# Beacon attention and soft MoE: V brought in four keys to a partition and put in order by matrix products

## The chip, the cores and the metric

The kernel runs on one core of a Trainium2 chip. The metric is the device time of one execution in microseconds (us); lower is better. Times are compared as medians of several executions.

## The reference

Attention comes first, for 8 batches and 8 heads of 576 queries with 64 elements each. 16 beacon keys, which every query sees, stand ahead of 576 causal keys. The result, as 4608 tokens of 512 elements, goes through a soft mixture of 8 experts with 4 slots each.

```python
k_all = np.concatenate([beacon_k, k], axis=2)          # 592 keys
v_all = np.concatenate([beacon_v, v], axis=2)
scores = scale * np.matmul(q, k_all.transpose(0, 1, 3, 2))
causal[:, Nb:] = np.triu(np.ones((S, S), dtype=bool), k=1)
a = np.exp(scores - scores.max(-1, keepdims=True)) ; a /= a.sum(-1, keepdims=True)
x = np.matmul(a, v_all)                                 # heads side by side: 4608 x 512
logits = x @ phi                                        # 4608 x 32 slots
d = softmax(logits, over tokens) ; slot_input = d.T @ x
slot_out[e] = np.maximum(slot_input[e] @ w1[e], 0.0) @ w2[e]
out = softmax(logits, over slots) @ slot_out
```

All inputs and the output are float32. Q, K, V and the beacons are 29 MB, the expert weights 33.5 MB, the output 9.4 MB.

## The kernel before

**Pairs.** The work is 32 pairs of heads, n = 0 to 31, four to a batch. g is n % 4 and b is n // 4. The order inside a pair is written out by hand: `order` (L472) gives a list of steps for each g, with other lists for the first two and the last three pairs, and `do` (L492) issues a step. S0 to S3 are the four steps of scores of a pair (`score`, L306). Each writes one of two PSUM buffers `sc0` and `sc1` in turn, and ScalarE takes the exponential of it into the tile `ex` (L319). S0 belongs to the next pair. A0 and A1 (`attend`, L334) multiply the exponentials of the pair before with V, for its two heads; after A1 VectorE takes the reciprocal of the sums (`r`, L348) and scales the result into `xb` (L349). T (`transp`, L284) transposes Q and K of pair n + 2 with 36 products of 64x64 into two buffers of the PSUM pool `tr`, which has two buffers in all; VectorE copies them out as `qT` and `kT` (L293). X01, X23 and X4 transpose `xb` of the batch before, L0 and L1 make its logits (L391, exponential on ScalarE at L395), D turns the exponentials (`dt_piece`, L425), SI sums the slots (L441, L454). All of these borrow buffers of `tr` as well.

**V.** `load_r` (L117) brings a batch's V in two loads of 128 partitions with two neighbouring keys to a partition, that is pieces of 512 bytes; the beacon rows are loaded over the first eight partitions (`load_bv`, L136) once the load below them has landed. The last 80 keys come on their own (`load_vl`, L140). GpSimd casts to float16 (`cast_r`, L354). Partition p of a chunk holds keys 2p and 2p + 1, so the scores read every other column of kT (`ks` in `steps`, L60), and the diagonal of the first 256 keys is folded: eight products of 64x64 in S0, a copy `vd` of half of V with zeros beside it (`dup`, L360, VectorE), two products per head against `vd` that are 130 columns wide, and a mask by a minimum with `fmask` (`mask_f`, step M, L331, VectorE). The other masks run on GpSimd (L303).

**Weights.** GpSimd issues 37 loads that cast to float16 (`load_w`, L156, issue at L171). `want(n)` (L540) says how many have been issued by the end of pair n: 0.68 n up to pair 24, and then a table. The last ten are halves that go into the buffers of Q and K when these come free.

**Start and queue.** SyncE issues the loads of Q and K of pairs 0 to 4, of the beacon keys, and of V at L181 to L200; later ones at L565 to L578. It works in order, and a load that has to wait holds up those behind it.

**End.** After the last pair come the logits of the last batch, the slot sums, layer one of two groups of four experts (`layer1`, L634), `turn` (L655), and layer two (`layer2`, L668) with 64 products of 512 columns that add up in one PSUM bank; 32 columns of weights at a time, so that four lie beside each other. Between the last pairs of products of layer two stand products whose result nobody reads (`idle_work`, L488, L688). Then `soh` (L690) is scaled, and 36 products, scalings and stores write the output (L695).

Of the kernel before, what the change touches and what calls it, by code (L numbers as in the profile page):

```python
# [17 lines left out]
def kernel(  # L18
# [13 lines left out]
    P = 128  # L32
# [21 lines left out]

    def f_(s):
        return [(64 * r, 64, 2 * P * r + s, 2, 2 * P * r, P, P * s) for r in range(2)]

    steps = [  # L60
        f_(0) + f_(1) + [(0, P, 2 * P, 2, 3 * P, U - 3 * P, 2 * P)],
        [(0, P, 2 * P + 1, 2, 3 * P, U - 3 * P, 0), (0, UL, 4 * P, 1, 4 * P, UL, 208)],
        [(0, P, 0, 2, P, U - P, 0)],
        [(0, P, 1, 2, P, U - P, 0)],
# [4 lines left out]
    XF, XG1, XT, XG0 = (0, P), (2 * P, 464), 672, (752, 1216)  # L69

    POS = [0, 2, 1, 3, 4]
    prods = [(P, XF[0], P, 0, 0, 2)] + [(P, XG0[s] + P, P, s, 1, 1) for s in range(2)]
    prods += [(P, XF[1], P, 1, 0, 2)]
    prods += [(P, XG0[s], P, s, 2, 1) for s in range(2)]
    prods += [(P, XG0[s] + 2 * P, P, s, 3, 1) for s in range(2)]
    prods += [(P, XG1[s], P, 2 + s, 3, 1) for s in range(2)]  # L80
    prods += [(P, XG0[s] + 3 * P, UL, s, 4, 1) for s in range(2)]
    prods += [(P, XG1[s] + P, UL, 2 + s, 4, 1) for s in range(2)] + [(UL, XT, UL, 4, 4, 1)]
    first, final = {0, 4, 6, 10}, {3, 5, 9, 14}
# [29 lines left out]

    vr, vl = {}, {}
    vrows = v.rearrange("b h s d -> (b h s) d")

    def load_r(b, r):  # L117
        t = vrp.tile([P, H, 2 * D], FP, name="vr", tag="vr")
        vr[(b, r)] = t
        o = b * H * S + 2 * P * r - Nb  # L120
        if b == 0 and r == 0:
            nc.sync.dma_start(
                out=t[:, 1:H, :], in_=vrows[S - Nb:S - Nb + (H - 1) * S].rearrange(
                    "(h s) d -> h s d", s=S)[:, 0:2 * P, :].rearrange(
                        "h (p t) d -> p h (t d)", t=2))
            nc.sync.dma_start(
                out=t[Nb // 2:P, 0, :],
                in_=v[0, 0, 0:2 * P - Nb, :].rearrange("(p t) d -> p (t d)", t=2))
        elif r == 0:
            nc.sync.dma_start(out=t[:, :, :], in_=vrows[o:o + H * S].rearrange(  # L130
                "(h s) d -> h s d", s=S)[:, 0:2 * P, :].rearrange("h (p t) d -> p h (t d)", t=2))
        else:
            nc.sync.dma_start(out=t[:, :, :], in_=v[b, :, 2 * P - Nb:4 * P - Nb, :].rearrange(
                "h (p t) d -> p h (t d)", t=2))

    def load_bv(b):  # L136
        nc.sync.dma_start(out=vr[(b, 0)][0:Nb // 2],
                          in_=beacon_v[b].rearrange("h (p t) d -> p h (t d)", t=2))
# [53 lines left out]
    load_bk(1, B)  # L192
    load_pair(2)
    load_r(0, 1)
    load_vl(0)
    load_bv(0)
# [13 lines left out]
    fmask = const.tile([P, 2 * P], F16, name="fmask")  # L210
    fm = const.tile([P, 2, P], F16, name="fm")
    nc.gpsimd.memset(fm[:, :, :], 65504.0)
    for base, lo in ((P, 64), (0, 0)):
        nc.gpsimd.affine_select(out=fm[:, :, :], in_=fm[:, :, :], compare_op=AL.is_ge,
                                fill=0.0, base=base, pattern=[[-1, 2], [1, P]],
                                channel_multiplier=-2)
        nc.gpsimd.tensor_copy(out=fmask[lo:lo + 64, :].rearrange("p (s t) -> p s t", s=2),
                              in_=fm[lo:lo + 64, :, :])
# [5 lines left out]
    for i in range(2):  # L224
        nc.gpsimd.memset(vh[i][:, :, :, D:DD], 1.0)


    vd = [const.tile([P, 2, 2, H, DD], F16, name=f"vd{i}") for i in range(2)]
    for i in range(2):
        nc.vector.memset(vd[i][:, :, :, :, :], 0.0)  # L230
    hTz = vd[0][:, :, :, :, :].rearrange("p s r h d -> p (s r h d)")
# [74 lines left out]
    def score(n, st):  # L306
        if st == 0:
            ex[n] = exq.tile([P, 2, EW], F16, name="ex", tag="ex")
        sc = scs[st % 2]
        for (p0, kn, k0, ks, u0, un, col) in steps[st]:  # L310
            for a in range(2):
                nc.tensor.matmul(  # L312
                    sc[p0:p0 + kn, a, col:col + un],
                    kT[n % 3][64 * a:64 * a + 64, k0:k0 + ks * (kn - 1) + 1:ks],
                    qT[n % 3][64 * a:64 * a + 64, u0:u0 + un],
                    start=True, stop=True)
        w, o = width[st], soff[st]
        x = ex[n]
        nc.scalar.activation(x[:, :, o:o + w], sc[:, :, 0:w], AF.Exp, scale=scale)  # L319

        if st == 0:
            mask(x[:, :, XG1[0]:XG1[0] + P], [[0, 2], [1, P]], P, -2)
        if st == 1:
            mask(x[:, :, XG1[1]:XG1[1] + P], [[0, 2], [1, P]], P - 1, -2)
            mask(x[0:UL, :, XT:XT + UL], [[0, 2], [1, UL]], 0, -1)
        if st >= 2:
            mask(x[:, :, XG0[st - 2]:XG0[st - 2] + P], [[0, 2], [1, P]], P + 2 - st, -2)

    def mask_f(n):
        x = ex[n][:, :, 0:2 * P]  # L330
        nc.vector.tensor_tensor(out=x, in0=x, in1=fmask[:, :].unsqueeze(1).broadcast_to(  # L331
            [P, 2, 2 * P]), op=AL.min)

    def attend(n, a):  # L334
        b, g = divmod(n, H // 2)
        h = 2 * g + a
        for j, (kn, o, m, c, pos, w) in enumerate(prods):
            dst = avs[0:m, a, pos * DD:(pos + w) * DD]
            if w == 2:
                dst, rhs = dst.rearrange("p (r d) -> p r d", r=2), vd[b % 2][:, c, :, h, :]  # L340
            else:
                rhs = vh[b % 2][0:kn, c, h, :]
            nc.tensor.matmul(dst, ex[n][0:kn, a, o:o + m], rhs,  # L343
                             start=j in first, stop=j in final)
# [9 lines left out]
    def cast_r(b, r, eng):  # L354
        eng.tensor_copy(  # L355
            out=vh[b % 2][:, 2 * r:2 * r + 2, :, 0:D].rearrange("p s h d -> p h s d"),
            in_=vr.pop((b, r))[:, :, :].rearrange("p h (s d) -> p h s d", s=2))

    def dup(b, r):
        nc.vector.tensor_copy(out=vd[b % 2][64 * r:64 * r + 64, :, r, :, :],  # L360
                              in_=vh[b % 2][0:64, 2 * r:2 * r + 2, :, :])
# [7 lines left out]
    def xt_piece(b, cs):  # L369
# [3 lines left out]
        for ii, i in enumerate(cs):  # L373
            m = P if i < 4 else UL
            for t in range(NDC):
                nc.tensor.transpose(  # L376
                    tp[:, ii, t, 0:m],
                    xb[b % 2][0:m, POS[i], 2 * t:2 * t + 2, :].rearrange("p h d -> p (h d)"),
# [23 lines left out]
    def xt_pair(g):  # L402
        tp = ps_tr.tile([P, NCH, P], F16, name="tr", tag="tr")
        for i in range(NCH):
# [3 lines left out]
                xb[(B - 1) % 2][0:m, POS[i], 2 * g:2 * g + 2, :].rearrange("p h d -> p (h d)"),  # L408
# [27 lines left out]
    def si_piece(b):  # L436
        sp = ps_tr.tile([P, NDC, NSL], FP, name="tr", tag="tr")
        for t in range(NDC):
            for i in range(NCH):
# [3 lines left out]
                    xb[b % 2][0:m, POS[i], 2 * t:2 * t + 2, :].rearrange("p h d -> p (h d)"),  # L443
# [6 lines left out]
    def si_moving(b):  # L450
        sp = ps_tr.tile([P, Dm], FP, name="tr", tag="tr")
        for i in range(NCH):
# [3 lines left out]
                xb[b % 2][0:m, POS[i], :, :].rearrange("p h d -> p (h d)"),  # L456
# [15 lines left out]
    order = ["d1 S1 A0 L1 M S2 A1 S3 cl T S0 D", "S1 A0 X01 M S2 SI A1 S3 T S0",  # L472
# [19 lines left out]
    def do(n, w):  # L492
# [32 lines left out]
        elif w[0] == "c" or w[0] == "d":  # L525
# [8 lines left out]
            else:  # L534
                dup(vb, int(w[1]))


    wl = 0

    def want(n):  # L540
# [203 lines left out]
```

## Time and profile before

| | |
|---|---|
| median of 3 runs | 213.84 us (213.62 to 214.66) |
| the profiled execution's own time | 214.08 us |
| its span, first to last instruction | 212.3 us |
| mean granted clock of TensorE | 0.955 |
| busy: PE, DVE, ACT, POOL | 166.0, 141.5, 127.4, 116.2 us |
| moved by DMA | 55.86 MB |

PE is TensorE, PEld its weight loads, DVE VectorE, ACT ScalarE, POOL GpSimd, SP SyncE; a q behind a name means the queue in front of the engine. A group line gives the line of the kernel, the engine, the operation, output and inputs, the number of instructions, then busy time and the mean of one in ns, and then the idle time ahead of it. The chain of waits is followed back from the last instruction; "issue" in it is time in which an engine waited for nothing that the profile shows. The durations of PE rows are latencies of a pipeline, so the time that a product takes from its neighbours is read from the starts, not from the durations.

### The profile page before, as it was taken

The page shows a single profiled execution, that of the slowest core. Times are in us where ns is not written, and L with a number is a line of the kernel's source. Part 1 is how long each engine was busy: PE and PEld are TensorE (multiplying, and loading weights), DVE is VectorE, ACT ScalarE, POOL GpSimd, SP SyncE. Part 2 cuts the span into 40 slices and gives each one's busy share as a digit, 9 for nine tenths or more (in the row PEclk, how much of TensorE's full clock was granted, in tenths as well). Part 3 has the DMA queues.
Part 4 walks back from the last instruction along what each step waited for, and adds up shares of the span by engine and source line. Part 5 has one row for each costly group of instructions (what it writes and reads, how often), then busy time and mean ns, then how long its engine had stood idle before and what let it go on. Part 6 is the DMA issues. An engine that isn't in the chain of part 4 may idle for free.

```text
span 212.3 us, 7656 instructions
## 1 busy us (share of the span) xinstructions
PE 166.0 (78%) x3276; PEld 110.7 (52%) x3276; DVE 141.5 (67%) x289; ACT 127.4 (60%) x179; POOL 116.2 (55%) x278
## 2 busy tenths in 40 slices
PE   2353999997899898689999789899899889888000
PEld 2232776765676576467666556666667542233000
DVE  5766489894798799279979678877855230299200
ACT  2154499795688778477978677688682210199100
POOL 7137179695658938556985676899887200000000
PEclk9999999996999999799999999999999999999855
DMA  6999899999999999999999999999999994089995
GB/s 191 294 267 342 275 286 277 275 278 280 299 246 285 269 266 305 298 282 290 296 271 242 289 287 260 244 209 212 211 211 212 210 209 75 0 297 415 415 412 240
DMA packets 44968, 55.86 MB, mean 263 GB/s; under 512 B 9103, under 2 KB 25991, under 8 KB 44935
## 3 DMA queue, kind: packets, MB, share of 16 engines
q1 hardware_dynamic: 36151, 38.60, 58.0%
q0 software_dynamic: 8784, 16.78, 42.5%
q8 instruction: 25, 0.41, 0.8%
q14 instruction: 8, 0.07, 0.1%
HBM read 62.71 MB, written 9.44 MB: 340 GB/s over the span
## 4 chain that ended last, share of the span: by engine, by line
PE 52%; DVE 15%; issue 8%; POOL 7%; DMA 6%; ACT 2%; SPq 1%; DVEq 0%; ACTq 0%; POOLq 0%
PE av L343 17%; PE sc L312 12%; PE tr L291 6%; DVE osb L708 4%; PE tr L391 4%; DVE xb L349 3%; DMA vr<-in_beacon_v_dram 3%; PE tr L376 3%; POOL ex L303 3%; DMA vr<-in_v_dram 3%; DVE qT L293 3%; PE av L671 3%; POOL vh L355 2%; PE sc L490 2%; POOL w L171 2%
## 5 line engine op out<-in xcount | busy, mean ns | idle before, releaser
L319 ACT ACTIVATE ex<-sc 128x928 f16<-128x928 f32 (+1 forms) x128 | 107.6, 869 | 42.0 <-PE sc L312 38.7
L303 POOL TENSOR_SCALAR_AFFINE_SELECT ex<-ex 128x256 f16<-128x256 f16 (+1 forms) x160 | 62.2, 406 | 44.1 <-ACT ex L319 42.7
L312 PE MATMUL sc<-qT,kT 64*64 64x128 bf16 (+3 forms) x576 | 52.4, 270 | 4.7 <-issue 2.7
L343 PEld LDWEIGHTS <-ex 128*128 128x128 f16 (+2 forms) x960 | 42.4, 109 | 16.7 <-issue 12.1
L343 PE MATMUL av<-vh,ex 128*128 128x65 f16 (+2 forms) x832 | 46.0, 202 | 0.7 <-issue 0.2
L312 PEld LDWEIGHTS <-kT 64*64 64x64 bf16 (+2 forms) x576 | 20.9, 104 | 18.9 <-issue 11.8
L349 DVE TENSOR_TENSOR xb<-av,r 128x640 f16<-128x640 f32 x32 | 26.4, 824 | 1.1
L343 PE MATMUL av<-vd,ex 128*128 128x130 f16 x128 | 23.4, 232 | 3.3 <-DVE vd L360 3.3
L293 DVE COPY kT<-tr 128x576 bf16<-128x576 bf16 x32 | 24.0, 748 | 2.0 <-PE tr L291 2.0
L293 DVE COPY qT<-tr 128x576 bf16<-128x576 bf16 x32 | 23.9, 748 | 1.6 <-PE tr L291 1.6
L291 PE MATMUL tr<-idb,kf 64*64 64x64 bf16 x576 | 16.4, 199 | 4.9 <-issue 4.2
L171 POOL DMA_DIRECT2D w<-in_moe_w_dram x27 | 19.4, 721 | 0.0
L291 PE MATMUL tr<-idb,qf 64*64 64x64 bf16 x576 | 16.2, 201 | 3.8 <-DMA qf<-in_q_dram 3.8
L705 ACT ACTIVATE osb<-fp,rc 128x512 f32<-128x512 f32 x18 | 11.3, 684 | 13.1 <-PE fp L703 12.4
L291 PEld LDWEIGHTS <-qf 64*64 64x64 bf16 x576 | 12.5, 114 | 10.2 <-issue 5.3
L355 POOL CAST vh<-vr 128x1024 f16<-128x1024 f32 x15 | 15.8, 1052 | 3.0 <-DMA vr<-in_beacon_v_dram 3.0
L331 DVE TENSOR_TENSOR ex<-ex,fmask 128x512 f16<-128x512 f16 x32 | 15.6, 487 | 2.6 <-ACT ex L319 2.3
L291 PEld LDWEIGHTS <-kf 64*64 64x64 bf16 x576 | 13.3, 115 | 5.6 <-issue 5.4
L381 DVE COPY xT<-tr 128x1024 f16<-128x1024 f16 x14 | 9.7, 691 | 7.3 <-PE tr L376 7.3
L348 DVE RECIPROCAL r<-av 128x10 f32<-128x10 f32 x32 | 6.9, 214 | 11.3 <-PE av L343 10.7
L360 DVE COPY vd<-vh 64x1040 f16<-64x1040 f16 x16 | 8.7, 543 | 6.4 <-POOL vh L355 6.2
L708 DVE TENSOR_SCALAR osb<-fp,rc 128x512 f32<-128x512 f32 x18 | 12.3, 746 | 0.7 <-PE fp L703 0.7
(90 smaller groups left out, 156.7 us busy)
## 6 DMA issues: line engine op xcount, KB each, us to landing
w<-in_moe_w_dram POOLq DMA_DIRECT2D x27, 512.0 KB, 9.4
qf<-in_q_dram SPq DMA_DIRECT2D x32, 288.0 KB, 7.0
kf<-in_k_dram SPq DMA_DIRECT2D x32, 288.0 KB, 7.5
out_dram<-osb SPq DMA_DIRECT2D x16, 512.0 KB, 5.5
vr<-in_v_dram SPq DMA_DIRECT2D x15, 512.0 KB, 7.3
wx<-in_moe_w_dram POOLq DMA_DIRECT2D x10, 256.0 KB, 9.7
vl<-in_v_dram SPq DMA_DIRECT2D x8, 160.0 KB, 7.0
out_dram<-osb SPq DMA_DIRECT2D x4, 256.0 KB, 3.2
```

Of the source, the lines that this page charges most:

```text
L171: nc.gpsimd.dma_start(out=t[:, 0:1024 * len(hs)].rearrange("p (c f) -> p c f", f=1024), in_=src)
L291: nc.tensor.transpose(tp[po:po + 64, j, :], hi, idb[po:po + 64, po:po + 64])
L293: nc.vector.tensor_copy(out=dst[:, Nb:Nb + S].rearrange("p (s j) -> p s j", j=J), in_=tp[:, :, :].rearrange("p j s -> p s j"))
L303: nc.gpsimd.affine_select(out=x, in_=x, compare_op=AL.is_ge, fill=0.0, base=base, pattern=pattern, channel_multiplier=cm)
L312: nc.tensor.matmul(sc[p0:p0 + kn, a, col:col + un], kT[n % 3][64 * a:64 * a + 64, k0:k0 + ks * (kn - 1) + 1:ks], qT[n % 3][64 * a:64 * a + ...
L319: nc.scalar.activation(x[:, :, o:o + w], sc[:, :, 0:w], AF.Exp, scale=scale)
L331: nc.vector.tensor_tensor(out=x, in0=x, in1=fmask[:, :].unsqueeze(1).broadcast_to([P, 2, 2 * P]), op=AL.min)
L343: nc.tensor.matmul(dst, ex[n][0:kn, a, o:o + m], rhs, start=j in first, stop=j in final)
L349: nc.vector.tensor_tensor(out=xb[b % 2][:, :, 2 * g:2 * g + 2, :].rearrange("p i a d -> p a i d"), in0=avv[:, :, :, 0:D], in1=r5[:, :, :]. ...
L355: eng.tensor_copy(out=vh[b % 2][:, 2 * r:2 * r + 2, :, 0:D].rearrange("p s h d -> p h s d"), in_=vr.pop((b, r))[:, :, :].rearrange("p h (s ...
L705: nc.scalar.activation(osb[:, j - j0, :], fp_[:, :], AF.Copy, scale=rc[:, i:i + 1])
L708: nc.vector.tensor_scalar(out=osb[:, j - j0, :], in0=fp_[:, :], scalar1=rc[:, i:i + 1], scalar2=None, op0=AL.mult)
```

## The change

V comes in four keys to a partition, half of the heads at a time (r is now the half): 60 and 64 partitions in two loads with pieces of 1 KB, and four partitions of beacons, which no longer overlap with the rest. The cast goes into a new tile `vc`. `v_order` takes it from there: for each of four chunks of 128 keys it adds up four products of 32 rows by 512 columns with the 0/1 tile `vsel`, two chunks in turn into the two buffers of `tr`, and VectorE (ScalarE for one of each two in pairs 0 and 1) copies them to `vh`. With the keys in order, the scores read kT without a stride, the mask M, `fmask`, `vd` and `dup` go, S0 has four products instead of ten, `attend` has fifteen products of 65 columns per head, and GpSimd has four masks a pair instead of five, the first twice as wide. In a batch's lists, c0 and c1 (casts) stand at g = 1 and 2 for the next batch, V01 at g = 3 between S2 and A1, V23 at g = 0 of the batch itself at the same place.

At the start V is loaded ahead of pair 2; the beacon keys of the other batches come after pair 2, and their cast and transposes (BC, BT) move from pair 0 to pair 1. Later loads of V are asked for by a table. `want` is one higher in most pairs up to 24. At the end, layer one and `turn` are interleaved, the unread products between the products of layer two go, `soh` is made in two halves, and the first output tile is made and stored in two halves. The diff, cut to its core:

```diff
     steps = [
-        f_(0) + f_(1) + [(0, P, 2 * P, 2, 3 * P, U - 3 * P, 2 * P)],
-        [(0, P, 2 * P + 1, 2, 3 * P, U - 3 * P, 0), (0, UL, 4 * P, 1, 4 * P, UL, 208)],
-        [(0, P, 0, 2, P, U - P, 0)],
-        [(0, P, 1, 2, P, U - P, 0)],
+        [(P, 0, 0, P, 0), (P, 2 * P, 2 * P, U - 2 * P, P)],
+        [(P, 3 * P, 3 * P, U - 3 * P, 0), (UL, 4 * P, 4 * P, UL, 208)],
+        [(P, 0, P, U - P, 0)],
+        [(P, P, P, U - P, 0)],
     ]
+    base = [soff[2] - P, soff[3] - P, P - 2 * P, soff[1] - 3 * P, soff[1] + 208 - 4 * P]
+    prods = [(j, c, 0 if j == 0 else base[c] + P * j) for j in range(NCH) for c in range(j + 1)]
...
     def load_r(b, r):
-        t = vrp.tile([P, H, 2 * D], FP, name="vr", tag="vr")
...
+        t = vrp.tile([P, HH, 4 * D], FP, name="vr", tag="vr")
+        hs_ = slice(r * HH, (r + 1) * HH)
+        for lo, hi in ((Nb // 4, 64), (64, P)):
+            nc.sync.dma_start(out=t[lo:hi, :, :], in_=v[b, hs_, 4 * lo - Nb:4 * hi - Nb, :]...)
+        nc.sync.dma_start(out=t[0:Nb // 4], in_=beacon_v[b, hs_]...)
...
     load_r(0, 0)
-    load_bk(1, B)
-    load_pair(2)
     load_r(0, 1)
     load_vl(0)
-    load_bv(0)
+    load_pair(2)
+    load_bk(1, B)
...
-    vd = [const.tile([P, 2, 2, H, DD], F16, name=f"vd{i}") for i in range(2)]
-    for i in range(2):
-        nc.vector.memset(vd[i][:, :, :, :, :], 0.0)
+    vc = const.tile([P, 4, H, D], F16, name="vc")
...
         if st == 0:
-            mask(x[:, :, XG1[0]:XG1[0] + P], [[0, 2], [1, P]], P, -2)
+            mask(x[:, :, 0:2 * P].rearrange("p a (i t) -> p a i t", i=2),
+                 [[0, 2], [0, 2], [1, P]], 0, -1)
+        if st == 1 or st == 3:
+            mask(x[:, :, o:o + P], [[0, 2], [1, P]], 0, -1)
...
+    def v_order(b, cs, engs):
+        tp = {c: ps_tr.tile([P, 512], FP, name="tr", tag="tr") for c in cs}
+        for t in range(4):
+            for c in cs:
+                nc.tensor.matmul(tp[c][:, :], vsel[32 * c:32 * c + 32, t, :],
+                                 vc[32 * c:32 * c + 32, t, :, :].rearrange("p h d -> p (h d)"),
+                                 start=t == 0, stop=t == 3)
+        for c, eng in zip(cs, engs):
+            o, i = vh[b % 2][:, c, :, 0:D], tp[c][:, :].rearrange("p (h d) -> p h d", d=D)
+            if eng is nc.scalar:
+                nc.scalar.activation(o, i, AF.Copy)
+            else:
+                eng.tensor_copy(out=o, in_=i)
...
-    order = ["d1 S1 A0 L1 M S2 A1 S3 cl T S0 D", "S1 A0 X01 M S2 SI A1 S3 T S0",
-             "S1 A0 X23 X4 M S2 A1 S3 c0 T S0", "d0 S1 A0 L0 M S2 A1 S3 c1 T S0"]
+    order = ["S1 A0 L1 cl S2 V23 A1 S3 T S0 D", "S1 c0 A0 X01 S2 SI A1 S3 T S0",
+             "S1 c1 A0 X23 X4 S2 A1 S3 T S0", "S1 A0 L0 S2 V01 A1 S3 T S0"]
-    lists[0] = "M BC S1 S2 BT c0 S3 d0 S0 cl".split()
-    lists[1] = "S1 M T0 c1 S2 d1 A0 S3 A1 S0 T".split()
+    lists[0] = "S1 c0 S2 c1 S3 V01 S0 cl".split()
+    lists[1] = "S1 V23 T0 S2 A0 S3 A1 S0 BC BT T".split()
+    lists[2] = "S1 A0 S2 c0 A1 S3 T S0".split()
+    lists[3] = "S1 A0 c1 S2 A1 S3 V01 T S0".split()
...
-            return int(0.68 * n)
+            return int(0.68 * n + 0.7)
...
-    hs0 = layer1(0)
...
+    for hf in range(2):
+        layer1(0, scs[0][:, hf, :], hf)
+    for hf in range(2):
+        relu(hs[0], scs[0][:, hf, :], hf)
+    layer1(1, hp1[0], 0)
+    turn(0, hs[0])
+    layer1(1, hp1[1], 1)
...
     for e in range(EG, E):
-        for t in range(0, NFC, 2):
-            layer2(e, (t, t + 1))
-            if e >= E - 2 and (e, t) != (E - 1, NFC - 2):
-                idle_work(spare, 2)
+        layer2(e, range(NFC))
...
-    nc.vector.tensor_scalar(out=soh[:, :], in0=sop[:, :], scalar1=rd[:, 0:1],
-                            scalar2=None, op0=AL.mult)
+    for hf in range(2):
+        nc.vector.tensor_scalar(out=soh[:, hf * HD:(hf + 1) * HD], in0=sop[:, hf * HD:(hf + 1) * HD],
+                                scalar1=rd[:, 0:1], scalar2=None, op0=AL.mult)
...
+                w = HD if i == 0 else Dm
+                for o in range(0, Dm, w):
...
```

## The prediction

> **What bounds the kernel now.** I read the page's slices first, then the busy time of four stretches, the chain of waits, one pair in the timeline, and the waits by engine.
>
> ```profile
> PEclk9999999996999999799999999999999999999855
> DMA  6999899999999999999999999999999994089995
> ```
>
> The transfers are at nine tenths or more from the second slice to about 177 us, pause for layer two, and are full again for the output. So the last weights, and behind them the output, can't come much earlier, whatever the engines do. Is that the only limit? The next answer, whose columns are the stretch, its length, busy time of PE, PEld, DVE, ACT and POOL, granted clock, DMA share and GB/s, has two mishaps and, in its last line, a batch without one.
>
> ```profile
> 47.40:48.90 1.50, 0.04 (x3) 0.00 (x0) 0.99 (x2) 0.50 (x1) 1.31 (x4) 1.00 1.11 261
> 49.70:53.10 3.40, 3.40 (x38) 2.35 (x36) 1.24 (x3) 2.75 (x5) 1.42 (x4) 0.50 1.11 279
> 84.20:86.90 2.70, 0.02 (x3) 0.01 (x2) 1.59 (x3) 0.03 (x1) 1.41 (x2) 1.00 1.09 359
> ...
> 53.60:70.26 16.66, 15.80 (x379) 11.47 (x379) 14.61 (x29) 13.89 (x20) 12.41 (x29) 1.00 1.10 285
> ```
>
> The clean batch takes 16.66 us with PE busy for 15.80, DVE for 14.61, ACT for 13.89: TensorE runs through its list with hardly a gap, VectorE is close behind. The other batches take up to 20.9 us, because PE stands still and then runs at half clock. The chain names it (start, length, what):
>
> ```profile
> 9.22 6.93 DMA vr<-in_beacon_v_dram
> ...
> 47.44 1.49 issue
> ...
> 84.22 2.68 issue
> ...
> 117.32 1.56 issue
> ...
> 177.69 0.54 PE sc L490 x2
> ```
>
> First the beacon rows of V hold up the start, then there are three stops that no semaphore explains, and from 177.69 the unread products carry the end. One pair (g = 2 into g = 3) in the timeline (start, length, engine, line):
>
> ```profile
> 98.69 0.37 PE L312 MATMUL sc<-qT,kT 64*128 64x464 bf16 x2
> ...
> 98.99 0.23 PE L343 MATMUL av<-vd,ex 128*128 128x130 f16 x1
> 99.06 0.22 PE L343 MATMUL av<-vh,ex 128*128 128x65 f16 x2
> ...
> 99.65 0.37 PE L312 MATMUL sc<-qT,kT 64*128 64x464 bf16 x2
> ...
> 101.06 0.13 PEld L312 LDWEIGHTS <-kT 64*128 64x128 bf16 x3 [0.17 <-issue]
> ...
> 102.58 0.41 ACT L395 ACTIVATE eLh<-tr 128x288 f16<-128x288 f32 x1
> 102.77 0.71 POOL L171 DMA_DIRECT2D w<-in_moe_w_dram  x1
> 102.78 0.23 PE L343 MATMUL av<-vd,ex 128*128 128x130 f16 x1
> ```
>
> S2 starts at 98.69 and A1 0.30 later, S3 at 99.65, and S1 of the next pair only at 101.06, 1.41 after S3, since it needs `sc1` back from the exponential of S3. In the waits, `PE tr L430 <- DVE qT L293: 3.2, 6, 0.5` shows that step D, at the end of g = 0, already stands half a microsecond for a `tr` buffer.
>
> **The change in the loop.** A batch gains V01 and V23, eight products of 512 columns each.
> - *Their streaming.* Four products of 288 columns take 0.49 (chain, PE tr L391 x4), so 512 columns take 0.218. S2's two products of 464 columns run side by side on 64 rows each: 0.198 of stream and 0.10 of changeover make the 0.30 above. If 32-row products pair up like that, a V is 4 x 0.218 + 0.10 = 0.97; one by one it is 8 x 0.218 + 0.10 = 1.84. The 64-row pair is the nearest row: 0.97.
> - *Their buffers.* V takes both buffers of `tr`, and the second belongs to L0 or L1, which stand just ahead. The logits' exponential starts at 102.58 and with its read of the sum ends at 103.08, while A1, where V would start, stood at 102.78. So the second chunk, and in order the rest, waits 0.3: V = 1.27, two make 2.5.
> - *VectorE.* M (487 ns) and dup (543) leave, 4 x 0.487 + 2 x 0.543 = 3.0 a batch; four copies of 128x512 from PSUM come, at the 692 ns of L651, 2.8. The sum is even, the place is not: both copies of a V stand ahead of `r` and `xb`, and A1 is only 0.6 long, so `r` comes some 0.6 late. A0 of the next pair has 0.46 of slack (xb over at 104.61, A0 at 105.07) and loses 0.1; D, which has none, loses 0.5. Together 0.6 a batch (0.1 to 1.4).
> - *What is saved.* A product against `vd` takes 0.07, one against `vh` 0.03 (98.99 to 99.06, then two to 99.12); two of 15 per head, so 0.12 a pair, 0.5 a batch (0.3 to 0.7). S0 falls from ten products to four, but T and S0 lie inside the 1.41 that ACT sets: nothing. GpSimd loses one mask in five and has one twice as wide (0.41, so 0.41 to 0.82), its casts keep their 1.05; with 12.41 of 16.66 busy it hides them.
>
> A batch: 2.5 + 0.6 - 0.5 = +2.6 (1.3 to 3.5). V23 of pair 4 and six full batches up to pair 28 make 6.5 of them: **+16.9** (8.5 to 23).
>
> **The start.** V is ahead of pair 2 and no longer waits for a landing, and 2 x 1.79 of memsets leave VectorE, which held qT of pair 0 until 6.84. But V01 needs both casts (GpSimd's after the masks of S1), then PE at half clock (T takes 0.69 there, 0.48 later), so V01 and V23 cost about 1.9 each, and T of pair 2 queues behind V23's copies. I get the first `attend` at 19.3 instead of 21.09. Then BC and BT, which filled a pause in pair 0, stand in pair 1 between S0 and T: PE waits for r, xb and 1.14 of casts, about 1.9. In pair 3 V01 stands between S3 and T, and its copies hold back T, 1.5. -1.8 + 1.9 + 1.5, less 0.6 for a clock that warms sooner: **+1** (-3 to +3.5).
>
> **The stops.** 1.49 + 2.68 + 1.56 and twice 3.4 us at half clock (1.7 lost each) are up to 9.1. They fall where the DMA share is 1.09 to 1.11. A batch of 19.3 with the same bytes leaves DMA pauses, so some should go; half is my choice: **-4** (-9 to 0). In pair 25 three weight loads are issued in a row instead of four (2.43 for four ahead of the masks): **-0.7** (-2 to 0). Pieces of 1 KB instead of 512 bytes: I count nothing, since the loop would be slower than the transfers.
>
> **The end.** From 177.69 to 183.73 there are 14 unread products and 14 of layer two; 32 of the latter take 1.84 (173.84 to 175.68), 14 then 0.8: -5.2. With `turn` beside layer one, the relu and copy between 172.4 and 173.84 are covered: -1.4 (-2 to -0.5). Halves of `soh` (0.76 whole) and a half first tile: -0.5. What is late next is the weights: the last was issued at 168.4 and takes 9.7, so 178.1; they are tied to the pairs, move with them, and one is issued earlier, so I take them as ready within 0.3. **-7** (-8 to -5).
>
> A rule bears on this. Row: stops of 1.5 and 2.7 us were followed by 3.4 us at clock 0.50, the one of 1.56 was not. The Trainium skill (TensorE: Matmul & The Clock Gate, Part 1) says that an idle window of about 3.4 us brings half rate; by it, dropping products that keep PE awake can cost where weights are late. Here that is a wait ahead of layer two's second half: 1.84 at half clock is 1.8 more, one chance in ten, inside the range.
>
> **Sum**, against the profiled execution's own 214.08 (span 212.3 and 1.8 around it; the median of the runs, 213.84, is 0.1% lower): 214.1 + 16.9 + 1 - 4 - 0.7 - 7 = 220.3, so **220**.
>
> The same Trainium skill page (Part 3, Measured speedup vs the span model) gives 3.07 times for four products of 32 rows and 512 columns side by side. An estimate from its 77% per place: 1.13 instead of 0.87 of stream for a V, 13 V, +3.4, and the sum would be 224. No row here shows 32-row products beside each other.
>
> **Rivals.**
> - *Faster: DMA makes the stops and paces the loop.* For it: the full DMA row, and that the stops lie where nothing else waits. Against: the clean batch at the same share (1.10). Here a pause in the transfers ends all stops, and the V products cost 1.9 a batch because no buffer is late: 214.1 + 12.4 - 9 - 0.7 - 8 - 0.8 at the start = 208. It decides if a batch costs under (9 + 0.7 + 7) / 6.5 = 2.6. Chance 0.20.
> - *V products one by one.* For it: every row that pairs does so on halves of 64 rows or quarters of columns. A V is 1.84 with the buffer's wait inside: +0.57, 13 times, 228. Chance 0.13.
> - *No change within what can be measured:* stops, end and loop cancel, 213 to 215. Chance 0.07.
> - That V at the head of the queue does not bring the start forward is in the start's range.
>
> **Chances.** Forecast 0.60 (215.5 to 226), rivals as above. The measurement can tell about 0.5% from no change: faster 0.20, same 0.07, slower 0.73. The range 209 to 228 leaves out half of the fast rival and the upper half of the slow one, under 0.2.
>
> **What would show it.** Right: clean batches of 19 us or more, S2 to A1 near 1.5 in g = 0 and 3, V's second chunk waiting for ACT eLh, D waiting over 1 us, DMA slices below nine, layer two in one piece. Wrong: V under 1 us with `r` not late, batches of 17 us, or V pairs that start a full 0.2 apart.

## The result and the profile after

The changed kernel takes **227.26 us** (median of four runs, 226.86 to 232.91) where the kernel before takes 213.73: a ratio of **1.064 [1.054, 1.074]**. The forecast was 220, slower by 2.9%; measured are 6.4%. The sign and the cost of a batch were right, the size was not. The ratios leave out disturbed runs, such as that of 232.91.

The profiled execution took 226.97 us with a span of 225.3. The reciprocal behind A1 (`r`) marks one point in every pair; the third row is from the last one, behind the last pair, to the end of the span:

| | before | after | difference |
|---|---|---|---|
| first `r` behind pair 4 (in pair 5) | 38.83 | 50.67 | **+11.8** |
| from there to the last `r` | 124.02 | 132.05 | **+8.0** |
| from the last `r` to the end | 49.43 | 42.55 | **-6.9** |

The first answer to look at is the slices of the changed kernel.

```profile
PEclk9999999569999999999999999999999999999955
DMA  6999999999989999999999999999999999559996
```

The two falls of the clock that stood in the middle of the kernel before are gone, and one fall of two slices, from 39 to 49 us, has come. A batch (columns as before: stretch, length, busy time of PE, PEld, DVE, ACT and POOL, clock, DMA share, GB/s) now is

```profile
70.28:89.70 19.42, 18.43 (x368) 11.89 (x366) 14.37 (x29) 14.34 (x20) 11.61 (x26) 1.00 1.08 260
```

19.42 instead of the clean 16.66. Counted from `r` to `r` the first five batches behind pair 5 take 19.4 to 20.0, the sixth, with the burst of weights, 21.05. The place where V01 stands, in the timeline of the changed kernel:

```profile
77.01 0.37 PE L274 MATMUL sc<-qT,kT 64*128 64x464 bf16 x2
77.11 0.41 ACT L357 ACTIVATE eLh<-tr 128x288 f16<-128x288 f32 x1
77.31 1.37 PE L315 MATMUL tr<-vc,vsel 32*128 32x512 f16 x8
...
78.53 1.29 DVE L323 CAST vh<-tr 128x512 f16<-128x512 f32 x2 [1.92 <-PE tr L315]
...
78.62 0.67 PE L295 MATMUL av<-vh,ex 128*128 128x65 f16 x15
```

V01 holds PE for 1.31 (77.31 to 78.62). The eight products start at 77.313; 77.668 and 77.674; 77.883 and 77.900; 78.098 and 78.116; 78.313. So two lie beside each other, 0.215 a pair, and the second chunk starts 0.355 late, after the logits' exponential has left its `tr` buffer. In the chain of waits the start and the end look like this (start, length, what):

```profile
25.55 1.06 DVE bk L232 x2
...
26.66 0.94 PE tr L237 x7
...
34.55 0.56 POOL ex L265
...
35.13 0.72 POOL w L140
35.85 0.21 POOL kT L260
36.06 0.63 POOL ex L265 x2
36.68 0.99 POOL vc L307
...
37.72 1.07 PE tr L315 x8
...
192.78 1.73 PE av L626 x32
...
195.18 1.94 PE av L626 x32
```

From 25.55 to 28.56 the beacon casts (BC), the transposes (BT) and their copies are the chain. From 34.55 on V01 of batch one waits for GpSimd, which has masks, the issue of a weight and a copy of kT ahead of the second cast `vc`. PE has been without work for 1.9 us, since 35.8. Layer two at the end is in two short pieces.

The windows behind the slow start follow. The recorded changes of the clock lie on a grid of 3.41 us; before its first record (32.1) the clock column shows 1.00, but the pairs of V products start 0.427 apart there, so it was half.

```profile
15.08:18.49 3.41, 3.39 (x22) 1.24 (x22) 0.69 (x1) 1.58 (x3) 0.08 (x1) 1.00 1.06 361
35.56:38.97 3.41, 1.28 (x10) 0.53 (x9) 1.22 (x3) 1.23 (x2) 2.46 (x6) 1.00 1.07 235
38.97:42.39 3.42, 2.87 (x59) 2.44 (x58) 2.52 (x4) 0.97 (x2) 0.00 (x0) 0.50 1.17 214
42.39:45.80 3.41, 3.41 (x28) 1.49 (x26) 0.90 (x2) 1.45 (x2) 1.98 (x5) 0.50 0.84 236
45.80:49.21 3.41, 3.41 (x65) 2.63 (x64) 2.67 (x5) 2.08 (x3) 0.53 (x2) 0.50 1.10 228
```

After the wait for V01 (PE busy for 1.28 of 3.41) the clock falls for three windows, 10.24 us. The middle one is full of products, and still the clock does not rise behind it.

Two theories were put up. **Order**: the start is long because BC, BT and V01 now stand on the path, and because the clock falls in the waits. **Transfers**: it is long because V's loads are slow and everything else comes late. For the second speaks that a piece of 1 KB takes 76 ns (median of the packets from 40 to 150 us), while two pieces of 512 bytes took 2 x 27.

### The profile page after: what moved, and what is told of

Read it like the earlier page. It is cut to its first block, busy times and chain, and to the rows that moved or that the text cites. A ratio compares the mean times of both kernels' runs of the same rounds, so it can differ in the third digit from the quotient of the medians.

```text
span 225.3 us, 7494 instructions
## 1 busy us (share of the span) xinstructions
PE 181.4 (81%) x3199; PEld 113.8 (51%) x3199; DVE 135.9 (60%) x270; ACT 129.7 (58%) x182; POOL 109.9 (49%) x246
## 4 chain that ended last, share of the span: by engine, by line
PE 56%; DVE 16%; POOL 7%; ACT 5%; issue 4%; DMA 4%; SPq 2%; DVEq 0%; ACTq 0%
PE av L295 15%; PE sc L274 12%; PE tr L315 9%; PE tr L253 7%; ACT ex L280 4%; DVE vh L323 4%; DMA vr<-in_v_dram 4%; DVE osb L672 4%; DVE xb L301 3%; PE tr L353 3%; POOL ex L265 3%; PE tr L338 2%; POOL w L140 2%; DVE qT L255 2%; POOL vc L307 2%
## 5 line engine op out<-in xcount | busy, mean ns | idle before, releaser
L265 POOL TENSOR_SCALAR_AFFINE_SELECT ex<-ex 128x256 f16<-128x256 f16 (+2 forms) x128 | 55.3, 445 | 72.5 <-ACT ex L280 70.8
L295 PE MATMUL av<-vh,ex 128*128 128x65 f16 (+2 forms) x960 | 48.9, 203 | 2.2 <-POOL ex L265 2.0
L274 PE MATMUL sc<-qT,kT 64*128 64x464 bf16 (+4 forms) x384 | 47.0, 304 | 2.0 <-DVE kT L260 0.9
L323 DVE CAST vh<-tr 128x512 f16<-128x512 f32 x30 | 19.5, 689 | 32.5 <-PE tr L315 32.5
L315 PE MATMUL tr<-vc,vsel 32*128 32x512 f16 x128 | 23.2, 421 | 5.2 <-DVE vc L307 3.1
L274 PEld LDWEIGHTS <-kT 64*128 64x128 bf16 (+1 forms) x384 | 15.9, 101 | 16.0 <-issue 10.1
L140 POOL DMA_DIRECT2D w<-in_moe_w_dram x27 | 19.4, 720 | 0.0
L669 ACT ACTIVATE osb<-fp,rc 128x512 f32<-128x512 f32 (+1 forms) x19 | 12.0, 664 | 6.7 <-PE fp L667 6.4
L307 POOL CAST vc<-vr 128x1024 f16<-128x1024 f32 x15 | 15.4, 1030 | 0.0
L315 PEld LDWEIGHTS <-vsel 32*128 32x128 f16 x128 | 6.7, 97 | 16.5 <-issue 13.7
L667 PE MATMUL fp<-soh,eLh 128*128 128x512 f16 (+1 forms) x37 | 10.8, 372 | 2.2 <-DVE soh L652 0.6
```

The source lines that it names most:

```text
L140: nc.gpsimd.dma_start(out=t[:, 0:1024 * len(hs)].rearrange("p (c f) -> p c f", f=1024), in_=src)
L265: nc.gpsimd.affine_select(out=x, in_=x, compare_op=AL.is_ge, fill=0.0, base=base, pattern=pattern, channel_multiplier=cm)
L274: nc.tensor.matmul(sc[0:kn, a, col:col + un], kT[n % 3][64 * a:64 * a + 64, k0:k0 + kn], qT[n % 3][64 * a:64 * a + 64, u0:u0 + un], start= ...
L295: nc.tensor.matmul(avs[0:m, a, j * DD:(j + 1) * DD], ex[n][0:kn, a, o:o + m], vh[b % 2][0:kn, c, h, :], start=c == 0, stop=c == j)
L307: eng.tensor_copy(out=vc[:, :, r * HH:(r + 1) * HH, :].rearrange("p s h d -> p h s d"), in_=vr.pop((b, r))[:, :, :].rearrange("p h (s d) - ...
L315: nc.tensor.matmul(tp[c][:, :], vsel[32 * c:32 * c + 32, t, :], vc[32 * c:32 * c + 32, t, :, :].rearrange("p h d -> p (h d)"), start=t == ...
```

## The experiments

**The end alone, e1_end.** The kernel before with only the end's part of the change:

```diff
-        for t in range(0, NFC, 2):
-            layer2(e, (t, t + 1))
-            if e >= E - 2 and (e, t) != (E - 1, NFC - 2):
-                idle_work(spare, 2)
+        layer2(e, range(NFC))
...
+    layer1(1, hp1[0], 0)
+    turn(0, hs[0])
+    layer1(1, hp1[1], 1)
```

> The kernel before with the end's part of the change alone (no unread products in layer two, turn beside layer one, soh and the first tile in halves). Theory of the prediction: 7 us less, 206.7, with layer two in one piece of 64 products (about 3.7 us instead of 9.9) and soh some 7 us sooner. Rival: the last weights, which land at 178.1, hold up layer two's second half, and the clock falls in the wait: 2 to 3 us less, 211.

Measured: 209.64, ratio 0.983 [0.974, 0.991]. In the profiled execution, 209.87, the end is 47.55 instead of 49.43, and its chain shows what is next:

```profile
168.78 9.74 DMA wx<-in_moe_w_dram
```

The last half weight lands at 178.52, and one lands every 1.25 us ahead of it. The rival of the expectation holds: 1.9 us at the end; the rest of this execution's gain lies in the loop (121.67 instead of 124.02), whose code is the same. Since that part differs from run to run, the same kernel ran again in five rounds:

> e1_end once more, in five rounds: the end's part of the change alone in the kernel before. If the 0.983 of the first time holds, it is 0.975 to 0.99; if it was the spread of the stops (the profiled execution had 2.4 us fewer of them up to pair 31), 0.99 to 1.0, since the end itself is held by the last weights.

Ratio 0.977 [0.971, 0.982]; the first finding stands. It is the fastest of the kernels that leave nothing out, and it beats both. How much of that is the end and how much the stops stays open: in the execution that was profiled here, the longest of its runs (213.31), the end was 45.86, 3.6 less than before, and the loop 127.79, 3.8 more.

**The unread products put back, e12_unread**, in the changed kernel:

```diff
-        layer2(e, range(NFC))
+        for t in range(0, NFC, 2):
+            layer2(e, (t, t + 1))
+            if e >= E - 2 and (e, t) != (E - 1, NFC - 2):
+                idle_work(spare, 2)
```

> The changed kernel with the unread products in layer two's second half put back (14 of them, as before). Theory of the prediction: they cost their own 5.2 us, 232. Rival 'the last weights, which land at 195.3, 1.8 us ahead of layer two's end, are what ends it': 1 to 3 us, 229.

233.47, ratio 1.105 [1.098, 1.111]; the end takes 48.13 instead of 42.55, +5.6. So the same 14 products cost their full time here, while in the kernel before most of it hid behind the weights: there the last one lands at 178.12, 15.3 behind the last `r`, in the changed kernel 12.6 behind it.

**V in one load of 128 rows, e2_v128:**

```diff
-        for lo, hi in ((Nb // 4, 64), (64, P)):
-            nc.sync.dma_start(out=t[lo:hi, :, :], in_=v[b, hs_, 4 * lo - Nb:4 * hi - Nb, :]...)
-        nc.sync.dma_start(out=t[0:Nb // 4], in_=beacon_v[b, hs_]...)
+        o = (b * H + r * HH) * S - Nb
+        nc.sync.dma_start(out=t[:, :, :], in_=vrows[o:o + HH * S]...[:, 0:4 * P, :]...)
+    def load_bv(b, r):      # asked for one or two pairs later
+        nc.sync.dma_start(out=vr[(b, r)][0:Nb // 4], in_=beacon_v[b, r * HH:(r + 1) * HH]...)
```

> The changed kernel with each half of V loaded over all 128 partitions in one load (the rows below the first one are read as well, and the beacon rows come over them afterwards, as before), pieces of 1 KB still. If the slow transfers come from loads that reach only 60 or 64 partitions, a piece of 1 KB takes about 46 ns (the lower tenth of those measured) instead of a median of 76; if they come from the size of the piece, it stays at 76. Theory 'transfers' (V's slow transfers made the start 11 us longer): 5 us or more less, below 222.5. Theory 'order' (where BC, BT and V01 of pair 3 stand, and the clock that falls there): 1 to 2 us less at the most, 225 to 227, for the wait of 3.1 for V's second half in pair 0.

A piece of 1 KB now takes 46 ns (median) instead of 76, and the 2304-byte pieces of Q and K beside it 93 instead of 106. The page of the profile shows the sum, the line of SyncE's queue in the changed kernel and then in e2_v128:

```profile
q1 hardware_dynamic: 27824, 38.35, 61.0%
```

```profile
q1 hardware_dynamic: 27867, 38.60, 49.5%
```

The same bytes take 49.5% of the engines' time instead of 61.0%. So it was not the size of the piece. This run makes one load of 128 partitions out of two, of 60 and 64, and doesn't tell the number of loads from the number of partitions. The Trainium skill (SBUF — State Buffer, Door 1: The DMA port swizzle) gives a reason for the latter: partitions 0 to 63 are reached through one half of 16 ports and 64 to 127 through the other. The 76 and 46 ns fit it; no run here shows the ports.

And the time: 228.01, ratio 1.067 [1.058, 1.075], the profiled execution 226.73, with `r` of pair 5 at 50.46. *Transfers* alone falls. One thing this run could not show: V's first half landed sooner (11.08), but the beacon rows on top of it at 13.98, so the first cast came no earlier than before.

**BC and BT covered, e3_bc:**

```diff
-    lists[1] = "S1 V23 T0 S2 A0 S3 A1 S0 BC BT T".split()
+    lists[1] = "S1 V23 T0 BC S2 A0 S3 BT A1 S0 T".split()
```

> The changed kernel with BC and BT of pair 1 beside other work (order S1 V23 T0 BC S2 A0 S3 BT A1 S0 T). Theory 'order': the 2.9 us from the start of BC (25.55) to the transposes of pair 2 (28.56) go, and the window with PE busy for 1.63 of 3.42 with them: pair 1 to pair 2 takes 4 to 5 us instead of 7.67, full clock may come sooner; in all 3 us less, 224, if the same time is not lost again in pair 3's wait for V. Theory 'transfers': nothing, 227, since pair 2 then waits for Q and K of pairs 2 and 4.

Pair 1 to pair 2 takes 2.7 instead of 7.7, and `r` of pair 5 comes at 43.17, 7.5 us sooner. Of that 1.9 is left at the last `r`, and the time is the same (228.39, ratio 1.073 [1.061, 1.084]; profiled execution 225.56). The chain of waits of e3_bc shows where it went:

```profile
58.56 11.00 DMA kf<-in_k_dram
...
77.12 12.26 DMA kf<-in_k_dram
...
89.44 12.32 DMA kf<-in_k_dram
```

A loop that starts earlier asks for K earlier than the slow loads let it through. Neither theory had this alone; both had half of it.

**Both together, e5_bc_v128:**

> BC and BT covered (as in e3_bc) and V loaded over 128 partitions (as in e2_v128) together. In e3_bc attends came 6.3 us sooner by pair 4 and 1.9 us sooner at the end: between them the loop stood where K landed 11 to 12.3 us after the chain turned to its load. Theory 'given back to the transfers': with V's pieces at 46 ns instead of 76 these waits go, the gain of the start stays, and the time is 4 to 5 us under the changed kernel, 222.5. Theory 'the stops are not the transfers': the same stops as in e3_bc, 225 to 228.

225.87, ratio 1.051 [1.043, 1.059]; profiled execution 223.45. From `r` of pair 5 to the last one it takes 131.67 instead of 137.66 in e3_bc: the waits for K are gone. But `r` of pair 5 comes at 46.66 and not at 43.17, since the clock is half for 10.24 us (35.0 to 45.3) where it was half for 3.41 in e3_bc. So by the medians 1.4 us went and not 4 to 5, and whether the loop is shorter only because it began later, this run can't say; e6_start can.

**V01 of batch one in pair 4, e4_v01:**

```diff
-    lists[3] = "S1 A0 c1 S2 A1 S3 V01 T S0".split()
+    lists[3] = "S1 A0 c1 S2 A1 S3 T S0".split()
+    lists[4] = "S1 A0 V01 cl S2 V23 A1 S3 T S0".split()
```

> The changed kernel with V01 of batch one in pair 4 (after A0) instead of pair 3 (ahead of T). Theory 'order': PE no longer stands from 35.5 to 37.7 for GpSimd's cast, no window of 3.41 us is left with PE busy for 1.29 only, and the 10.24 us at clock 0.50 go: 6 to 7 us less, 220.5. Theory 'transfers': 1 to 2 us less, and a wait for Q and K instead. A third outcome, the wait goes but the clock falls elsewhere: 2 us less.

Its runs lie between 224.39 and 234.89 and give no ratio. In the profiled execution (228.49) the third outcome seems to have come: pair 4 is 2.3 us sooner, but the clock was half from 26.9 to 33.7 and from 40.5 to 47.3. The first of these falls lies ahead of the moved V01, and e12_unread, whose start is that of the changed kernel, has it as well (27.4 to 34.2).

**The start put right, e6_start:** e5_bc_v128 with that V01, and the cast for it on VectorE at the head of pair 3:

```diff
-                cast_r(vb, int(w[1]), nc.vector if n == 0 and w == "c1" else nc.gpsimd)
+                cast_r(vb, int(w[1]), nc.vector if n in (0, 3) and w == "c1" else nc.gpsimd)
```

> e5_bc_v128, and V01 of batch one in pair 4, with the cast of its second half on VectorE at the head of pair 3 instead of GpSimd behind the masks. Theory 'order' for the start: no window is left in which PE is busy for under 2 of 3.41 us between pairs 1 and 5, full clock from about 24 us on, r of pair 5 (50.7 in the changed kernel, 38.8 before) at about 42; if the transfers do not give it back, 9 us less, 218. Rival: the loop starts sooner than Q and K can come, and the time is 222 or more, with K's landing in the chain of waits.

222.49, ratio 1.041 [1.031, 1.050]; profiled execution 219.69, with `r` of pair 5 at 43.07, as early as in e3_bc, and a loop as long as in the changed kernel (131.96 for 132.05), so nothing is given back. Without the slow loads, *order* carries 7.6 of the 11.8 us. But one window at half clock is left, behind this one; the second fence shows the V products' own part of it (stretch, length, busy time of PE and PEld, clock, DMA share, GB/s):

```profile
34.61:38.02 3.41, 2.90 (x29) 1.18 (x26) 1.77 (x3) 0.94 (x1) 1.15 (x3) 1.00 1.11 253
```

```profile
34.61:38.02 3.41, 2.27 (x15) 0.69 (x11) 1.00 1.11 253
```

PE was busy for 2.90 of 3.41, and the clock fell; with 2.54 it stays up in the same execution (58.50 to 61.91). Most of the 2.90 were products of 32 rows.

**Products of 32 rows and the clock, e8_rows128:**

```diff
-                nc.tensor.matmul(tp[c][:, :], vsel[32 * c:32 * c + 32, t, :],
-                                 vc[32 * c:32 * c + 32, t, :, :]...,
+                ro = slice(0, P) if b < 2 else slice(32 * c, 32 * c + 32)
+                nc.tensor.matmul(tp[c][:, :], vsel[ro, t, :], vc[ro, t, :, :]...,
```

> The changed kernel with the V products of batches 0 and 1 over all 128 rows instead of 32 (the sums of the four chunks are mixed, so V is wrong there); eight such products can't lie beside each other, so V01 and V23 take 3.4 us each at half clock instead of 1.9. Theory 'products of 32 rows do not count as busy for the clock': with full rows the clock rises after the first window of 3.41 us that is full of products, around 18.4 to 22 us instead of 32.1, and the second fall lasts one window (3.41) instead of three (10.24). Rival 'rows do not matter, the window before was not full': full clock not before 28, and two or three windows again.

```profile
14.86:18.27 3.41, 3.41 (x16) 1.16 (x15) 0.69 (x1) 1.56 (x3) 0.04 (x1) 1.00 1.08 343
```

Behind this window the clock is recorded as full, at 18.3 instead of 32.1, though the window of 15.08 in the changed kernel was as full. In the four other profiled executions with the same code up to there (e4_v01, e7_no_v, e12_unread, e13_fill) it becomes full at 22.9 to 24.5, behind the first full window without products of 32 rows. The first `r` comes at 22.9 instead of 24.5, with products that take longer; the whole, one execution, takes 226.94. Over all profiled executions up to 175 us, 57 windows at half clock (as it is taken to be before the first record) are filled for 3.39 us or more. In 43 of them products of 32 rows alone fill 0.37 or less, and the clock rose behind each; in 14 they fill 0.43 to 2.59, and it rose behind none.

**The clock by itself, e13_fill:** ten unread products ahead of V01 in pair 3 of the changed kernel, in the time in which PE waits.

```diff
-    lists[3] = "S1 A0 c1 S2 A1 S3 V01 T S0".split()
+    lists[3] = "S1 A0 c1 S2 A1 S3 I V01 T S0".split()
...
+        elif w == "I":
+            t = ps_tr.tile([P, 512], FP, name="tr", tag="tr")
+            for _ in range(10):
+                nc.tensor.matmul(t[:, :], idh[:, :], vsel[:, :, :]..., start=True, stop=True)
```

> The changed kernel with ten unread products of 128 rows and 512 columns ahead of V01 in pair 3, where PE stands for 2.2 us for GpSimd's cast (ten take 2.15). If the fall of the clock there costs by itself, the 10.24 us at clock 0.50 from 39 on go, and pairs 4 and 5 come 4 to 5 us sooner although no wait is shorter: 222.5, unless the loop gives it back to the landing of K as in e3_bc (225). If the clock only follows the late cast and costs nothing of its own, nothing: 227.

The fall at 39 is gone, and `r` of pair 5 comes at 47.59, 3.1 us sooner, although V01 waits no less. Of that, 0.6 is there before the unread products begin. The same code doesn't always start alike: `r` of pair 5 comes at 50.67 in the changed kernel, 48.29 in e7_no_v and 52.11 in e12_unread. So the fall is better read from `r` of pair 3 to that of pair 5: 12.67 instead of 15.13, 15.06 and 16.44, **2.4 to 3.8** less. The median of the time stays (226.82; 226.93 for the profiled execution), though its ratio, 1.050 [1.041, 1.060], is lower than the changed kernel's; the two did not run side by side. In the profiled execution the lead is still 2.5 in pair 25 and is lost up to pair 28. Three weights are issued in a row behind pair 25, the clock falls at 154.2, and in the window behind, which is full of products, 1.88 us of them V's alone, it does not rise (half until 161.0).

**Spreading V01 and V23, e14_spread,** was to keep up the clock in e6_start:

```diff
-    lists[3] = "S1 c1 A0 S2 A1 S3 T S0".split()
-    lists[4] = "S1 A0 V01 cl S2 V23 A1 S3 T S0".split()
+    lists[3] = "S1 c1 A0 S2 A1 S3 T V01 S0".split()
```

> e6_start with V01 of batch one at the end of pair 3 (after T) instead of beside V23 in pair 4. In e6_start the clock fell after a window in which PE was busy for 2.90 of 3.41 us, 0.76 of it with products of more than 32 rows. If products of 32 rows hardly count for the clock, spreading V01 and V23 over two windows keeps it up, and 1.5 us go: some 218.2 for the profiled execution's 219.7. If the fall in e6_start had another reason, the clock falls as before: 219.7 or a little more.

It failed as a test: V01 waited for the copies of T, PE was busy for only 1.66 of a window, 1.32 of it with products of 32 rows alone, and the fall behind it tells nothing of the rows (224.56, ratio 1.042 [1.034, 1.050]).

**V's price in the loop, e7_no_v and e11_start_no_v**, the same edit in the changed kernel and in e6_start:

```diff
-            else:
+            elif vb < 2:
                 v_order(vb, (0, 1) if w == "V01" else (2, 3), ...)
```

> The changed kernel without the products and copies of V01 and V23 from batch two on (loads and casts stay; the attends of these batches use the V of batches 0 and 1). Theory of the prediction: a clean batch takes 19.4 - 3.1 + 0 = 16.3 to 16.8 us instead of 19.42, and 5.5 to 6 batches give 15 to 17 us, if nothing else holds them: 211. Rival 'the transfers pace a faster loop': the batches go to 17.5 to 19 us with K's landing or stops in the chain, 217 to 222.

> e6_start without the products and copies of V01 and V23 from batch two on (these batches use the V of batches 0 and 1), as in e7_no_v. There batches of 16.3 us were followed by waits for K and V to land, and 5.5 of some 17 us were gained. Theory 'loads over half the partitions made those waits': with all 128 partitions the loop keeps 16.3 us a batch, and the time is 15 us or more under e6_start's 219.7: 203 to 205. Rival 'the transfers are full in either shape': K's landing or stops hold the loop, 210 to 215, about the kernel before.

e7_no_v: 225.19 (221.45 to 230.23), which gives no ratio; profiled execution 221.45. Its batches without a stop take 16.45 us, but the chain is full of landings of K and V of 9 to 18 us, and the clock falls three times in the loop: 5.5 us are left of some 17. e11_start_no_v: 207.64, ratio 0.982 [0.977, 0.986]; profiled execution 206.31, 13.4 under e6_start, 16.9 us a batch instead of 19.6 in the first five, and 16.44 instead of 19.43 in the clean ones. So V's products and copies cost 3.0 us in a clean batch, provided that the transfers can follow a faster loop; over the whole loop 15.2 of some 18 are left.

**Where the stops come from, e10_late_w:** the kernel before without weights up to pair 24.

```diff
         if n < 25:
-            return int(0.68 * n)
+            return 0
```

> The kernel before with no weights asked for up to pair 24; the rest of the table is as it was, so 20 loads are issued in a row at pair 25, and the end waits for weights (230 us or more; the time is not the point). Looked at are the pairs up to 24. Theory 'the stops need full transfers': the stops of 1.5 to 2.7 us near 47, 84 and 117 and the windows at clock 0.50 behind them are gone, and attends reach pair 24 about 8 us sooner than in the kernel before (r of pair 24 at 131.8 there). Rival 'the stops come from the instructions alone': they stay, at the same distance from the loads of instructions (16 KB each, at 46.7, 84.2 and 116.6 in the kernel before).

```profile
PEclk9999999999999999999999655555999999999955
DMA  6998989968678858857848999999999999939996
```

The five batches up to pair 25 take 16.6 us each, no stop is left, although loads of instructions still come every 4 to 8 us, and `r` of pair 25 comes at 121.61 instead of 131.84 (one execution, 238.81 in all). The kernel before loses 10.2 us to the weights' loads. The run takes out their issue on GpSimd together with their transfers; that the transfers do it is likely by the full DMA row, but not told apart.

**The end and earlier weights, e9_end_want:** e1_end with

```diff
-            return int(0.68 * n)
+            return int(0.68 * n + 0.7)
```

> e1_end (the kernel before with the end's part of the change) and, from the change too, the weights one load earlier (0.68 n + 0.7). In e1_end the last weights landed at 178.5 and layer two waited for them. Theory 'one burst shorter': three loads in a row in pair 25 instead of four, and the last weights some 1.2 us sooner: 1 us less than e1_end, some 208.5, or 0.976 of the kernel before. Rival 'the transfers are full from the second slice on, so a weight that comes earlier holds up K by as much': 0.98 as e1_end, or slower.

0.999 [0.994, 1.004], where e1_end had 0.983 and 0.977: by these ratios the whole gain is lost, though the two did not run side by side. The profiled execution, 215.07, is one of the longer of its runs (210.10 to 217.23); there pairs 27 to 29 take 8.4, 10.1 and 6.3 us, with landings of V in the chain. That a weight which comes earlier pushes V back in transfers that are full fits this, but is not shown for the shorter runs.

## Why the prediction was wrong

- **The step that failed is the start, "+1 (-3 to +3.5)"; it measured +11.8,** of which the forecast counts 1.3, V23 of pair 4, under the loop. Two more profiled executions with the same start (e7_no_v, e12_unread) give +9.5 and +13.3, as far outside. Its own terms: the first `attend`, "19.3 instead of 21.09", came at 21.87; with A1 that makes +0.6 instead of -1.8. "PE waits for r, xb and 1.14 of casts, about 1.9": 4.0 (pair 2 takes 7.67 instead of 3.70), since the transposes and copies behind the casts are on the path too. "In pair 3 V01 stands between S3 and T, and its copies hold back T, 1.5": 6.8 in that pair and 0.8 in the next, with V23 of pair 4 and, by e13_fill, some 2.5 of half clock inside; the stretch ahead of it gave 0.4 back. First came not the copies but GpSimd's cast behind masks and a weight's issue, which the prediction did not follow through that queue, and behind the wait the clock fell. With BC and BT covered and that cast and V01 moved, e6_start gives 7.6 of the whole back (6.3 in e11_start_no_v, whose start is the same).
- **"Less 0.6 for a clock that warms sooner" did not come.** It became full 6.3 us later (32.1 instead of 25.8) and fell again for 10.24 us. In the four other executions with that code it was full for the first time at 22.9 to 24.5, but for one window only, and then half again until 29.7 to 34.2. The fall behind V01 is worth 2.4 to 3.8 (e13_fill). The Trainium skill's section that the prediction weighed (TensorE: Matmul & The Clock Gate, Part 1) speaks of an idle window of 3.4 us; the grid agrees, but the windows that brought the clock down here had PE busy for 1.28 us, or 2.90 where products of 32 rows were most of it. The measurement decides. The prediction weighed the rule only at the end, where it didn't bite, and not in the start.
- **The loop, +2.6 a batch: right.** 19.42 less 16.66 is 2.76. Its terms are nearly so: V's products and copies, 2.5 + 0.6 = 3.1, cost 3.0 in a clean batch (19.42 and 19.43 against 16.45 and 16.44 in e7_no_v and e11_start_no_v), and what is saved, 0.5, was 0.2 (16.66 against 16.45). V01 is 1.31 (forecast 1.27), the second chunk 0.355 late (0.3), D waits up to 0.9, S2 to A1 is 1.61. Products that run one by one, the rival at 228, are refuted by their starts; the total close to 228 came from elsewhere.
- **The stops, -4, were right in direction and half in size; the burst, -0.7, brought nothing.** Six batches at 2.76 are 16.6; the loop from pair 5 is only 8.0 longer, so 8.6 went. The first five batches were 9.7 us over the clean batch before and are 1.0 over it now; the sixth, with the burst, was 1.3 over and is 1.6. By e10_late_w the weights' loads made the stops (10.2 up to pair 25); that a slower loop leaves the transfers time is argued, not tested. This is close to the fast rival's mechanism, which was given 0.20: the stops went, but a batch cost more than the 2.6 under which that rival would have decided.
- **The end, -7: 6.9,** but only behind a slower loop; by itself it is 1.9 in e1_end and 3.6 in e16_end_again, with the last weights next in e1_end, where the prediction took them as ready within 0.3.
- **"Pieces of 1 KB: I count nothing"** was right for the time as it stood, and wrong about the transfers: with the loads of 60 and 64 rows SyncE's queue takes 61.0% of the DMA engines' time, with loads of 128 rows 49.5%, and of the DMA slices below nine, named as a sign, the loop has one. It matters as soon as the start is mended (a loop of 137.66 in e3_bc against 131.96 in e6_start, with `r` of pair 5 at 43.2 and 43.1).
- **The sum:** 11.8 + 8.0 - 6.9 = 13.0, the difference of the spans. The forecast had 6.2: the start 9.5 too low, the loop (16.9 - 4 - 0.7 - 1.3 = 10.9) 2.9 too high.

What stays open: 4.2 us of the start that e6_start did not bring back. By `r`, 3.0 of them lie in the stretch that ends in pair 4, where V01 and V23 of batch one stand; one half-clock window (38.0 to 41.4) begins near its end. The runs do not divide it further. Open, too, is why executions of one start differ by up to 3.8 us at `r` of pair 5; where the grid of the clock lies against the waits differs among them.

## What to carry to other kernels

Follow a moved step through every queue that it joins, with what is already in it, and look at the start by itself: there waits are not hidden, and here a fall of the clock came on top of them. A saving is worth what the next limit leaves of it: here a slower loop lost its stops, the slow loads took away most of the start's gain, and the last weights hid most of the end's. So price a part both in the old surroundings and in the new ones.

## What the runs showed of the hardware

- Products of 32 rows hardly counted for the clock: 14 windows at half clock full of products, at least 0.43 us of them of that kind alone, did not raise it, and 2.90 us of which 2.27 were of that kind did not hold it.
- A window need not be idle to take the clock down: in the kernel before, 1.93 us of products in 3.41 (46.28 to 49.70) were too few; from 2.3 us of wider products on none fell up to 175 us. It is no sharp line: 1.89 held in e8_rows128 (35.34 to 38.76), 2.21 did not in e9_end_want (138.75 to 142.17).
- A piece of 1 KB took 76 ns (median) in pairs of loads into 60 and 64 partitions, and 46 in single loads into 128.
- Two products of 32 rows and 512 columns ran fully beside each other, 0.215 us for both; ten of 128 rows, one after the other, took 2.27 (e13_fill).
